# Tables and rows of the second and third expert asked for during the products of the expert before

## The chip, the core and the metric

The kernel runs on one core of a Trainium2 chip. The core has five engines that work from their own instruction streams and wait for each other on semaphores: PE (TensorE, matrix products; its weight loads are listed as PEld), DVE (VectorE), ACT (ScalarE), POOL (GpSimd) and SP (SyncE, which here only reads registers and issues DMAs). The metric is the device time of one execution in microseconds (us); less is better.

## The reference, cut to what matters

Attention with a small learned bias, then a dense MLP, then a mixture of experts with one expert for each token. Only the last part is touched by the change:

```python
def _moe2_ref(x, w_gate, w1, w2, capacity):          # x is 1152 x 512, 8 experts, capacity 288
    logits = x @ w_gate
    expert_idx = np.argmax(logits, axis=1)
    ...                                              # gate_w: softmax probability of the chosen expert
    for i in range(N):
        e = expert_idx[i]
        if counts[e] < capacity:
            disp[e, counts[e]] = x[i]
            ...
    h = np.maximum(np.einsum('ecd,edf->ecf', disp, w1), 0.0)     # 512 -> 1024
    y = np.einsum('ecf,efd->ecd', h, w2)                         # 1024 -> 512
    ...                                              # out[i] = gate_w[i] * y of the token's place, else 0
```

## The kernel before, in words

**Before the experts.** Attention and the dense MLP run in five row tiles, in an order written out in a list of numbers. They leave the MLP's output rows in a DRAM tensor `yscr` (1152 x 512), and a DRAM table `tbl` that gives, for each of the 8 experts and each of its 288 places, the token in the place and its gate weight. None of this is touched.

**The experts' order.** `experts_list` (DVE) makes a list `lst` of the experts that have tokens, with their count and the number `nf` of experts that are worked through in full. SP reads the list's entries into registers `ev[k]`, because the addresses of an expert's weights in DRAM depend on them. In this data the trace shows three experts worked in full (k = 0, 1, 2) and one more worked by a short path (`with_few`) beside the last.

**One expert, k.** `table(k)`: SP fetches the expert's 288 table entries into `tb` (96 x 3 x 2 numbers). `gather(k)`: DVE turns them into row numbers `gid`, and POOL issues three indirect DMAs, 96 rows of 2 KB each, from `yscr` into three tiles `XG`. `tokens(k)`: DVE makes the token numbers `tid` for the scatter at the end. `load1(k, i)` and `load2(k, i)`: SP fetches the two weight matrices in four pieces of 512 KB each, into `R1` and `R2` (shown as `AT` in the trace); a piece is fetched again for the next expert as soon as its last reader is done. `square`, `sized` and `halves` scale a piece by a power of two and split it into two float16 halves, `W1` and `W2`: the high half on ACT (on DVE for the fourth piece), the low half on DVE.

`gemm1(k)` is eight blocks of 12 matmuls (`ph`, `pt` <- `xT`, `W1`), with ACT and DVE making the two halves `HH` of each block's result. `gemm2(k)` is four blocks of 24 matmuls (`py` <- `HH`, `W2`). After its third block (dt = 2) PE turns the next expert's rows: `xt(k + 1, c)` transposes `XG[c]` into a bank, and ACT and DVE split that into `xT`, the moving operand of `gemm1(k + 1)`. `back` transposes a result back to rows, and `finish(k)`, which runs inside `gemm1(k + 1)`, ends it and issues the three scatters of the expert to `out` on POOL.

**What sets the order.** From the experts on there is no planner: each engine runs its instructions in the order of the code, `expert(0)` calling `gemm2(0)`, `expert(1)` calling `gemm1(1)`, `gemm2(1)` and so on, with a branch on `nf` between. Before the change, `table(k + 1)`, `gather(k + 1)` and `tokens(k + 1)` stand between `gemm1(k)` and `gemm2(k)`, and SP reads all of `ev[1]` to `ev[7]` and one more number ahead of `load1(1)`.

Of the kernel before, what the change touches and what calls it, by code (L numbers as in the profile page):

```python
# [25 lines left out]
E, F2 = 8, 1024  # L26
# [264 lines left out]
def tile_kernel(ctx: ExitStack, tc: tile.TileContext, a: dict, cap: int):  # L291
    nc = tc.nc
# [13 lines left out]
    def ts(eng, out, in0, s1, op0, s2=None, op1=ALU.bypass):  # L306
        eng.tensor_scalar(out=out, in0=in0, scalar1=s1, scalar2=s2, op0=op0, op1=op1)  # L307

    def stt(out, in0, s, in1, op0, op1, eng=None):
        (eng or dve).scalar_tensor_tensor(out=out, in0=in0, scalar=s, in1=in1, op0=op0, op1=op1)  # L310
# [36 lines left out]
    def cs(name, shape, dt=F32):  # L347
        return cst.tile(shape, dt, name=name)
# [841 lines left out]
    fl, lst, W = cs("fl", [1, E + 3]), cs("lst", [1, E + 3], I32), {}  # L1190
    ev = [None] * E

    def load1(k, ct):
        sp.dma_start(R1[:, ct], a["m1"][bass.ds(ev[k], 1), P * ct:P * ct + P].rearrange("o p f -> (o p) f"))

    def load2(k, i):
        sp.dma_start(RW2[:, 2 * i:2 * i + 2], a["m2"][bass.ds(ev[k], 1), 2 * P * i:2 * P * i + 2 * P].rearrange("o (c p) n -> p (o c) n", p=P))
# [7 lines left out]
    def raw(m, i):  # L1205
        return RW2[:, 2 * i:2 * i + 2] if m else R1[:, i]

    def sca(k, m, i, n=1):
        return W["s"][:, k % 2, m, i:i + n]

    def square(k, m, i, junk):
        j = junk.bitcast(BF16)
        act.activation(j.rearrange("p (a b) -> p a b", a=2) if m else j, raw(m, i), AF.Square, accum_out=sca(k, m, i))
# [188 lines left out]
    def table(k):  # L1402
        sp.dma_start(tb[k % 3], tv[bass.ds(ev[k], 1)].rearrange("o p c w -> (o p) c w"))

    def gather(k):
        g_ = gid[k % 3]
        ts(dve, g_, tb[k % 3][:, :, 0], float(NT - 1), ALU.min)
        for c in range(NCH):
            pool.indirect_dma_start(out=XG[c], out_offset=None, in_=yscr, in_offset=bass.IndirectOffsetOnAxis(ap=g_[:, c:c + 1], axis=0))

    def tokens(k):
        dve.tensor_copy(tid[k % 3], tb[k % 3][:, :, 0])

    def summed(k, m):
        tsum(sca(k, m, 4), sca(k, m, 0, 4))

    def sized(k, m, bank):
        total(k, m, bank)
        size(k, m, bank[:, 0:P])

    def halves(k, m, i):
        dst = W2[:, :, 2 * i:2 * i + 2] if m else W1[:, :, i]
        if i > 2:
            ts(dve, dst[:, 0], raw(m, i), sca(k, m, 5), ALU.mult)
        else:
            act.activation(dst[:, 0], raw(m, i), AF.Identity, scale=sca(k, m, 5))  # L1426
        stt(dst[:, 1], raw(m, i), sca(k, m, 5), dst[:, 0], ALU.mult, ALU.subtract)
# [6 lines left out]
    P3 = ((0, 0), (0, 1), (1, 0))  # L1434

    def gemm1(k, more=True, between=None):
        b_ = bool(k)
        for ft in range(8):
            ps = (PH + PT)[ft % 4]
            seq = [(ct, wv, xv) for ct in range(4) for wv, xv in P3]  # L1440
            for i, (ct, wv, xv) in enumerate(seq):
                pe.matmul(ps[:, 0:SL], W1[:, wv, ct, P * ft:P * ft + P], XT[k % 2][:, xv, ct], start=i == 0, stop=i == 11)  # L1442
            act.activation(HH[:, 0, ft], ps[:, 0:SL], AF.Relu)
            if k and ft == 0:
                summed(k, 1)
            stt(HH[:, 1, ft], ps[:, 0:SL], 0.0, HH[:, 0, ft], ALU.max, ALU.subtract)
            if k and ft == 0:
                finish(k - 1)
            if k and ft == 1:
                sized(k, 1, PO[0])  # L1450
            if ft > 1 and ft < 6:
                halves(k, 1, ft - 2)
            if k and more and ft > 3:
                square(k + 1, 0, ft - 4, W["j"])
            if between:
                between(ft)
# [10 lines left out]
    def gemm2(k):  # L1467
        if k == 0:
            for i in range(4):
                square(1, 0, i, W["j"])  # L1470
        summed(k + 1, 0)

        for dt in range(4):
            ps = PY[dt % 2]
            for ft in range(8):
                for i, (wv, hv) in enumerate(P3):
                    pe.matmul(ps[:, 0:SL], W2[:, wv, ft, P * dt:P * dt + P], HH[:, hv, ft], start=ft == 0 and i == 0, stop=ft == 7 and i == 2)  # L1477
            act.activation(YT[:, dt], ps[:, 0:SL], AF.Copy, scale=sca(k, 0, 7))
            if dt == (k == 0):
                sized(k + 1, 0, PO[1])  # L1480
            if dt == 2:
                for c in range(NCH):
                    xt(k + 1, c, (PT + PH)[c % 4])
            if dt == 1 or dt == 2:
                halves(k + 1, 0, 2 * dt - 2)
                halves(k + 1, 0, 2 * dt - 1)
            if dt > 0:
                back(k, dt - 1)
            if dt > 1:
                square(k + 1, 1, 2 * dt - 4, W["j"])  # L1490
                square(k + 1, 1, 2 * dt - 3, W["j"])

    def finish(k):
        back(k, 3)
        for c in range(NCH):
            scatter(k, c)
# [56 lines left out]
    def with_few(k):  # L1553
        few_loads()
        few_rows()
        if k:
            gemm1(k, False, lambda ft: few_x() if ft == 6 else None)
        else:
            few_x()

        def between(c):
            if c < 2:
                few_h(c)
            if c:
                few_flip(c - 1)
        gemm2_last(k, between)
        few_y(0)
        few_y(1)
        act.activation(XG[0], PO[1][:CS], AF.Copy, scale=sel[:, 0, 1:2])
        pool.indirect_dma_start(out=a["out"], out_offset=bass.IndirectOffsetOnAxis(ap=tidf[:, 0:1], axis=0), in_=XG[0], in_offset=None, bounds_check=NT - 1, oob_is_err=False)  # L1570

    def last(k):
        if k:
            gemm1(k, False)
        gemm2_last(k)

    def expert(k):
        if k + 1 == E:
            last(k)
            return  # L1580
        def next_():
            if k:
                for i in range(4):
                    load1(k + 1, i)
                gemm1(k)
            table(k + 1)
            gather(k + 1)
            tokens(k + 1)
            for i in range(4):
                load2(k + 1, i)  # L1590
            gemm2(k)
            expert(k + 1)

        def end():
            with tc.If(nv > k + 1) as more:
                with_few(k)
            with more.Else():
                last(k)

        if k < 2:  # L1600
            with tc.If(nf > k + 1) as more:
                next_()
            with more.Else():
                end()
        else:
            with tc.If(nf < k + 2) as done:
                end()
            with done.Else():
                next_()
# [2 lines left out]
    experts_list()  # L1612
    ts(dve, hm[:, 0:1], tok[:CS, 0:1], float(HC), ALU.is_lt)
    ts(dve, hm[:, 1:2], tok[:CS, 0:1], float(HC), ALU.is_ge)
    for k in range(1, E):
        ev[k] = nc.values_load(lst[0:1, k:k + 1], engines=[mybir.EngineType.SP], min_val=0, max_val=E - 1)
    evf = [nc.values_load(lst[0:1, E + 2:E + 3], engines=[mybir.EngineType.SP], min_val=0, max_val=E - 1)]
    for i in range(4):
        load1(1, i)
    gemm1(0)  # L1620
    tokens(0)
    nv = nc.values_load(lst[0:1, E:E + 1], min_val=1, max_val=E)
# [59 lines left out]
```

## Time and profile before

| | us |
|---|---|
| median of 3 runs (542.69 to 548.86) | 543.06 |
| the profiled execution, its own time | 543.5 |
| its span, first to last instruction | 541.6 |

| engine | busy us | share of the span |
|---|---|---|
| PE | 495.9 | 92% |
| DVE | 434.3 | 80% |
| ACT | 394.8 | 73% |
| POOL | 38.7 | 7% |

The mean granted clock of PE over the span is 0.962 of full speed. Times in the rows below are counted from the first instruction of the span. A busy PE is not a PE at its peak: matmuls are pipelined, and their ends are modelled, so spacings are read from starts.

### The profile page before, as it was taken

How to read it: one execution, taken by the hardware profiler on the slowest of the kernel's cores; microseconds unless marked ns; L12 is line 12 of the kernel's file. 1: busy time of each engine (PE TensorE's matmuls, PEld its weight loads, DVE VectorE, ACT ScalarE, POOL GpSimd, SP SyncE). 2: the span in 40 equal slices, each digit the busy share in tenths (PEclk: the TensorE clock that was granted, in tenths of full speed). 3: DMA queues.
4: the chain of work that ended last, by engine and by line, in shares of the span. 5: the costliest groups of instructions: out<-in, count | busy, mean ns of one | idle time of the engine just before them, and what ended most of it. 6: DMA issues, size and time to landing. Idle time of an engine off the chain costs nothing.

```text
span 541.6 us, 11894 instructions
## 1 busy us (share of the span) xinstructions
PE 495.9 (92%) x4479; PEld 336.9 (62%) x4479; DVE 434.3 (80%) x1172; ACT 394.8 (73%) x807; POOL 38.7 (7%) x67
## 2 busy tenths in 40 slices
PE   4756988999999999999999999999998797979994
PEld 3311655776676764566788747898467575867551
DVE  7999899999988899999877865799978966748300
ACT  7999999999875899999987633467952276847210
POOL 1000010000000011000000000001003002222101
PEclk9896699999999999999999999999999898999998
DMA  8998777630010233456331021180011267594100
GB/s 311 404 356 300 250 275 251 227 111 1 12 62 1 88 130 45 149 177 215 114 98 53 2 71 39 26 327 2 0 70 32 73 193 252 168 309 176 45 15 19
DMA packets 28211, 73.78 MB, mean 136 GB/s; under 512 B 4838, under 2 KB 4966, under 8 KB 26096
## 3 DMA queue, kind: packets, MB, share of 16 engines
q1 hardware_dynamic: 26576, 69.21, 37.7%
q0 software_dynamic: 1568, 3.72, 2.4%
q8 instruction: 37, 0.61, 0.5%
q14 instruction: 30, 0.25, 0.2%
HBM read 55.27 MB, written 17.87 MB: 135 GB/s over the span
## 4 chain that ended last, share of the span: by engine, by line
PE 57%; DMA 20%; DVE 11%; ACT 7%; issue 4%; SPq 1%; POOL 0%; another core or an unknown queue 0%; POOLq 0%; DVEq 0%; ACTq 0%
PE pb L868 15%; DMA xg<-yscr,gid 13%; PE pb L835 11%; PE pb L727 6%; PE ps L835 6%; DMA rw<-wi 4%; PE pb L663 3%; PE pb L518 3%; PE ps L633 3%; PE ps L663 2%; ACT ra L655 2%; ACT ra L666 2%; DVE WOt L310 1%; PE ps L619 1%; DMA out<-OC,tid 1%
## 5 line engine op out<-in xcount | busy, mean ns | idle before, releaser
L835 PEld LDWEIGHTS <-WIt 128*128 128x128 f16 x960 | 85.2, 98 | 10.6 <-issue 1.0
L835 PE MATMUL pb<-PX,WIt 128*128 128x256 f16 (+1 forms) x648 | 69.0, 263 | 0.0
L868 PE MATMUL pb<-WOt,ra 128*128 128x512 f16 x204 | 48.1, 379 | 0.0
L518 PE MATMUL pb<-ra,w2s 128*32 128x512 f32 (+17 forms) x252 | 37.4, 519 | 7.9 <-ACT ra L507 3.5
L868 PE MATMUL pb<-WOt,rw 128*128 128x512 f16 x180 | 42.0, 379 | 0.0
L655 ACT ACTIVATE ra<-ra,rm 128x576 f32<-128x576 f32 x50 | 39.3, 789 | 2.0 <-DVE rm L654 1.6
L507 ACT ACTIVATE ra<-AT,stab 128x512 f32<-128x512 f32 (+17 forms) x62 | 38.6, 663 | 2.1 <-DVE stab L307 2.0
L310 DVE SCALAR_TENSOR_TENSOR W<-AT,wsc,W 128x1024 f16<-128x1024 f32 x24 | 30.5, 1281 | 7.7 <-ACT W L1426 6.7
L868 PEld LDWEIGHTS <-ra 128*128 128x128 f16 x204 | 19.8, 98 | 22.2 <-issue 0.9
L654 DVE CUSTOM_DVE_ANT_0 ra<-ps,ra 128x576 f32<-128x576 f32 x43 | 31.3, 752 | 2.5 <-PE ps L622 1.4
L727 PE MATMUL pb<-ra,AT 128*64 128x128 f32 (+1 forms) x540 | 32.5, 271 | 0.7 <-ACT ra L666 0.7
L1442 PEld LDWEIGHTS <-W 128*128 128x128 f16 x288 | 28.1, 98 | 7.8 <-DVE xT L1186 1.0
L835 PE MATMUL ps<-PX,WIt 128*128 128x256 f16 (+1 forms) x312 | 32.8, 260 | 0.0
L1054 POOL DMA_INDIRECT tbl<-pk,rm x9 | 11.1, 1233 | 265.0 <-DVE rm L1051 175.8
L868 PEld LDWEIGHTS <-rw 128*128 128x128 f16 x180 | 17.3, 98 | 20.5 <-issue 1.4
L727 PEld LDWEIGHTS pb<-ra,AT 128*64 128x64 f32 x540 | 27.9, 139 | 3.3 <-ACT ra L666 1.4
L532 ACT ACTIVATE rbe<-pb,rl 128x48 f32<-128x48 f32 (+25 forms) x64 | 28.6, 484 | 1.4 <-DMA bscr<-rbe 0.6
L310 DVE SCALAR_TENSOR_TENSOR rw<-rw 128x1024 int32<-128x1024 int32 x24 | 29.3, 1224 | 0.0
L663 PE MATMUL pb<-ident,ra 128*128 128x128 f32 x159 | 24.0, 286 | 3.3 <-ACT ra L655 2.6
L1477 PE MATMUL py<-HH,W 128*128 128x288 f16 x192 | 26.9, 301 | 0.0
L666 ACT COPY ra<-pb 128x384 f32<-128x384 f32 x49 | 22.5, 492 | 3.5 <-PE pb L663 2.9
L307 DVE TENSOR_SCALAR ra<-AT,stab 128x544 f32<-128x544 f32 (+16 forms) x56 | 23.2, 445 | 0.9 <-PE pb L868 0.9
(477 smaller groups left out, 1155.2 us busy)
## 6 DMA issues: line engine op xcount, KB each, us to landing
AT<-m SPq DMA_DIRECT2D x24, 512.0 KB, 5.0
bscr<-rbe SPq DMA_DIRECT2D x36, 295.5 KB, 2.5
rw<-wo SPq DMA_DIRECT2D x8, 1024.0 KB, 6.2
ra<-bscr SPq DMA_DIRECT2D x28, 288.0 KB, 3.8
rw<-wi SPq DMA_DIRECT2D x4, 1024.0 KB
WOt<-wi SPq DMA_DIRECT2D x4, 1024.0 KB, 11.4
AT<-k SPq DMA_DIRECT2D x4, 576.0 KB
out<-ra SPq DMA_DIRECT2D x9, 256.0 KB, 2.7
```

The costliest lines, as they stand in the source:

```text
L310: (eng or dve).scalar_tensor_tensor(out=out, in0=in0, scalar=s, in1=in1, op0=op0, op1=op1)
L507: on_act = lambda h_=h_, g=g: act.activation(h_.t[:, 0:dn], T[:, 0:dn], AF.Relu, bias=stab[:, g:g + 1])
L518: pe.matmul(ps.t[32 * c:32 * c + 32, 0:d1 - d0], w2s, hs[c].t[:, d0:d1], start=True, stop=True)
L532: op("ACT", c_act(n, 1, 50), lambda ends=ends: act.activation(*ends(), AF.Copy, scale=rl[:, blk:blk + 1]), r=[ps, "stab"], p=[be], alt=[(" ...
L654: op("DVE", c_dve(S), lambda i=i, own=own, m_=m_, b_=b_: dve.tensor_tensor_reduce(out=own(), in0=blk(s_.t[:, 960 * i:960 * i + S]), in1=bl ...
L655: op("ACT", c_act(S, 2), lambda i=i, m_=m_, col=col: act.activation(t_.t[:, S * i:S * i + S], t_.t[:, S * i:S * i + S], AF.Exp, bias=m_.t[ ...
L663: pe.transpose(pa.t[:, P * j:P * j + P], t_.t[:, 384 * n + P * j:384 * n + P * j + P], ident)
L666: op("ACT", c_act(384, 0, 55), lambda dst=dst, src=src: act.copy(dst(), src()), r=[pa], w=[("tT", it, ct, b, n)], hold=[t_], alt=[("DVE", ...
L727: pe.matmul(ov[64 * i:64 * i + 64, ct % 2, w * bb:w * bb + w], v_, t_.t[:, at + c0:at + c0 + w], start=n == 0, stop=n == 4)
L835: pe.matmul(ps.t[:, n * f_:n * f_ + n], WI[:, wv, ct, P * ft:P * ft + P], xt.t[:, xv, ct, 0:n], start=i == 0, stop=i == 11)
L868: pe.matmul(y_.t, gv()[:, g2, c:c + P], WO[:, wv, ft], **kw)
L1442: pe.matmul(ps[:, 0:SL], W1[:, wv, ct, P * ft:P * ft + P], XT[k % 2][:, xv, ct], start=i == 0, stop=i == 11)
```

## The change

`table(1)` and `load1(1)` are issued right after the first number, `ev[1]`, is read; the other numbers are read behind them. `gather` now ends with `tokens`. `gather(1)` stands inside `gemm1(0)`, in its fourth block (ft = 3). For k = 1 and on, `table(k + 1)` stands ahead of `load1(k + 1)`, and `gather(k + 1)` at the head of `gemm1(k)`. In `gemm1(0)` alone the high half of the fourth piece of `W2` goes from DVE to ACT.

```diff
     def gather(k):
...
             pool.indirect_dma_start(out=XG[c], ...)
+        tokens(k)
...
     def halves(k, m, i):
-        if i > 2:
+        if k and i > 2:
             ts(dve, dst[:, 0], raw(m, i), sca(k, m, 5), ALU.mult)
...
     def gemm1(k, more=True, between=None):
+        if k and more:
+            gather(k + 1)
         for ft in range(8):
...
             act.activation(HH[:, 0, ft], ps[:, 0:SL], AF.Relu)
+            if k == 0 and ft == 3:
+                gather(1)
...
         def next_():
             if k:
+                table(k + 1)
                 for i in range(4):
                     load1(k + 1, i)
                 gemm1(k)
-            table(k + 1)
-            gather(k + 1)
-            tokens(k + 1)
             for i in range(4):
                 load2(k + 1, i)
             gemm2(k)
...
-    for k in range(1, E):
+    ev[1] = nc.values_load(lst[0:1, 1:2], ...)
+    table(1)
+    for i in range(4):
+        load1(1, i)
+    for k in range(2, E):
         ev[k] = nc.values_load(lst[0:1, k:k + 1], ...)
...
-    for i in range(4):
-        load1(1, i)
     gemm1(0)
```

On SP, where the second expert's table (`tb_5231`) and its weights (`AT<-m`) are asked for, the kernel before has this, behind the eight reads of the list and the four issues of `load1(1)`, whose last is the first row:

```order
L1194 DMA AT<-m 128x1024
L1622 TENSOR_LOAD lst
L1622 ISA x2
L1623 TENSOR_LOAD lst
L1623 ISA x2
L1601 COMPARE_AND_BRANCH
L1403 ISA
L1403 DMA tb_5231<-tbl 96x3x2
L1197 ISA
L1197 DMA AT<-m 128x2x512
```

and the change this, from the first table (`tb_5230`) on:

```order
L1403 DMA tb_5230<-tbl 96x3x2
L1616 TENSOR_LOAD lst
L1616 ISA x2
L1403 ISA
L1403 DMA tb_5231<-tbl 96x3x2
L1194 ISA
```

The table has moved ahead of seven reads of the list, the two reads for the branch, the branch itself and the four weight pieces; the pieces have moved ahead of seven reads.

On POOL, from the last scatter into `tbl` to the gathers for the third expert (`gid_5235`), the kernel before has

```order
L1054 DMA tbl<-pk_166,rm_126 2304x2
L1622 TENSOR_LOAD lst
L1623 TENSOR_LOAD lst
L1601 COMPARE_AND_BRANCH
L1409 DMA xg_5223<-yscr,gid_5234 96x512
L1409 DMA xg_5224<-yscr,gid_5234 96x512
L1409 DMA xg_5225<-yscr,gid_5234 96x512
L1601 COMPARE_AND_BRANCH
L1459 DMA out<-OC,tid_5236 1152x512 x3
L1409 DMA xg_5223<-yscr,gid_5235 96x512
L1409 DMA xg_5224<-yscr,gid_5235 96x512
L1409 DMA xg_5225<-yscr,gid_5235 96x512
```

and the change

```order
L1409 DMA xg_5223<-yscr,gid_5234 96x512
L1409 DMA xg_5224<-yscr,gid_5234 96x512
L1409 DMA xg_5225<-yscr,gid_5234 96x512
L1625 TENSOR_LOAD lst
L1626 TENSOR_LOAD lst
L1602 COMPARE_AND_BRANCH x2
L1409 DMA xg_5223<-yscr,gid_5235 96x512
L1409 DMA xg_5224<-yscr,gid_5235 96x512
L1409 DMA xg_5225<-yscr,gid_5235 96x512
L1462 DMA out<-OC,tid_5236 1152x512 x3
```

The first three gathers have moved ahead of the reads and the branch, the next three ahead of the first expert's scatters.

On DVE, in `gemm1(0)` from its third block (`pt_5221`) on, the kernel before has

```order
L310 SCALAR_TENSOR_TENSOR HH<-pt_5221,HH 128x288
L310 SCALAR_TENSOR_TENSOR W_5211<-AT,wsc,W_5211 128x1024
L310 SCALAR_TENSOR_TENSOR HH<-pt_5222,HH 128x288
L310 SCALAR_TENSOR_TENSOR W_5211<-AT,wsc,W_5211 128x1024
L310 SCALAR_TENSOR_TENSOR HH<-ph_5215,HH 128x288
L310 SCALAR_TENSOR_TENSOR W_5211<-AT,wsc,W_5211 128x1024
L310 SCALAR_TENSOR_TENSOR HH<-ph_5216,HH 128x288
L307 TENSOR_SCALAR W_5211<-AT,wsc 128x1024
L310 SCALAR_TENSOR_TENSOR W_5211<-AT,wsc,W_5211 128x1024
L310 SCALAR_TENSOR_TENSOR HH<-pt_5221,HH 128x288
```

and the change

```order
L310 SCALAR_TENSOR_TENSOR HH<-pt_5221,HH 128x288
L310 SCALAR_TENSOR_TENSOR W_5211<-AT,wsc,W_5211 128x1024
L307 TENSOR_SCALAR gid_5234<-tb_5231 96x3
L1413 CAST tid_5237<-tb_5231 96x3
L310 SCALAR_TENSOR_TENSOR HH<-pt_5222,HH 128x288
L310 SCALAR_TENSOR_TENSOR W_5211<-AT,wsc,W_5211 128x1024
L310 SCALAR_TENSOR_TENSOR HH<-ph_5215,HH 128x288
L310 SCALAR_TENSOR_TENSOR W_5211<-AT,wsc,W_5211 128x1024
L310 SCALAR_TENSOR_TENSOR HH<-ph_5216,HH 128x288
L310 SCALAR_TENSOR_TENSOR W_5211<-AT,wsc,W_5211 128x1024
L310 SCALAR_TENSOR_TENSOR HH<-pt_5221,HH 128x288
```

The two small instructions on the table stand between the third and the fourth block, and the 128x1024 `TENSOR_SCALAR` is gone from DVE.

## Rows read from the trace of the kernel before

**Rows 1.** Waits of PE from 429 us on: line, released by: us, times, longest.

```profile
PE pt L1431 <- DMA xg<-yscr,gid: 4.4, 4, 2.1
PE ph L1431 <- DMA xg<-yscr,gid: 1.2, 2, 0.9
...
PE po L1216 <- DVE wsc L327: 0.3, 1, 0.3
```

**Rows 2.** Timeline, PE, second expert's rows: start, us, what [idle before <-releaser].

```profile
448.27 3.10 PE L1477 MATMUL py<-HH,W 128*128 128x288 f16 x24
453.48 0.55 PE L1431 MATMUL pt<-ident,xg 96*128 96x96 f32 x4 [2.11 <-DMA xg<-yscr,gid]
454.38 0.55 PE L1431 MATMUL pt<-ident,xg 96*128 96x96 f32 x4 [0.35 <-DMA xg<-yscr,gid]
455.19 0.59 PE L1431 MATMUL ph<-ident,xg 96*128 96x96 f32 x4 [0.26 <-DMA xg<-yscr,gid]
455.57 0.84 PE L1464 MATMUL po<-ident,YT 128*96 128x128 f32 x3
456.21 4.46 PE L1477 MATMUL py<-HH,W 128*128 128x288 f16 x24
...
462.31 0.49 PE L1464 MATMUL po<-ident,YT 128*96 128x128 f32 x3
```

**Rows 3.** Timeline, PE, behind the third expert's rows.

```profile
487.99 3.95 PE L1477 MATMUL py<-HH,W 128*128 128x288 f16 x24
...
493.57 0.49 PE L1464 MATMUL po<-ident,YT 128*96 128x128 f32 x3
```

**Rows 4.** Windows: us, busy PE, PEld, DVE, ACT, POOL, PEclk, DMA, GB/s.

```profile
401.00:402.00 1.00, 0.53 (x6) 0.44 (x4) 0.50 (x3) 0.56 (x1) 0.00 (x0) 1.00 0.44 172
...
456.00:458.00 2.00, 2.00 (x10) 1.31 (x9) 1.23 (x3) 2.00 (x3) 0.00 (x0) 0.50 0.37 141
```

**Rows 5.** SP: reads of the list (last figures: first and last start), and DMA issues.

```profile
L1616 SPq TENSOR_LOAD <-lst x7: 262/266/289, 432.3 to 435.8; - x7
...
437.08 2.75 SPq L1194 DMA_DIRECT2D AT<-m  x4
441.31 0.33 SPq L1403 DMA_DIRECT2D tb<-tbl  x1
461.21 0.33 SPq L1403 DMA_DIRECT2D tb<-tbl  x1
```

**Rows 6.** The small tables (tile tb), three of them, from issue to landing.

```profile
DMA to landing us min/median/max: 3.2/4.2/5.3
```

**Rows 7.** The gathered rows (tile xg), from issue to landing.

```profile
DMA to landing us min/median/max: 2.4/5.7/8.3
```

**Rows 8.** Timeline, DVE and POOL, around the tables and the gathers.

```profile
435.61 1.28 DVE L310 SCALAR_TENSOR_TENSOR W<-AT,wsc,W 128x1024 f16<-128x1024 f32 x1 [0.58 <-ACT W L1426]
442.28 0.82 DVE L310 SCALAR_TENSOR_TENSOR HH<-pt,HH 128x288 f16<-128x288 f32 x2
446.60 0.17 DVE L307 TENSOR_SCALAR gid<-tb 96x3 uint32<-96x3 int32 x1 [3.44 <-DMA tb<-tbl]
447.72 0.92 POOL L1409 DMA_INDIRECT xg<-yscr,gid  x1 [25.93 <-DMA AT<-m]
473.24 1.80 POOL L1459 DMA_INDIRECT out<-OC,tid  x1 [3.65 <-DMA out<-OC,tid]
```

**Rows 9.** Timeline, ACT and DVE, between the waits and the next product.

```profile
451.96 0.50 ACT L1478 ACTIVATE YT<-py,wsc 128x288 f32<-128x288 f32 x1 [0.74 <-PE py L1477]
456.20 1.14 ACT L1426 ACTIVATE W<-AT,wsc 128x1024 f16<-128x1024 f32 x1
459.36 1.28 DVE L310 SCALAR_TENSOR_TENSOR W<-AT,wsc,W 128x1024 f16<-128x1024 f32 x1
482.72 0.50 ACT L1478 ACTIVATE YT<-py,wsc 128x288 f32<-128x288 f32 x1
487.98 1.14 ACT L1426 ACTIVATE W<-AT,wsc 128x1024 f16<-128x1024 f32 x1
```

More of the change, by code (lines that the diff above doesn't have):

```diff
@@ L1436, in gemm1 @@
     def gemm1(k, more=True, between=None):
-        b_ = bool(k)
+        if k and more:
+            gather(k + 1)
         for ft in range(8):
             ps = (PH + PT)[ft % 4]
-            seq = [(ct, wv, xv) for ct in range(4) for wv, xv in P3]
-            for i, (ct, wv, xv) in enumerate(seq):
+            for i, (ct, wv, xv) in enumerate([(ct, wv, xv) for ct in range(4) for wv, xv in P3]):
                 pe.matmul(ps[:, 0:SL], W1[:, wv, ct, P * ft:P * ft + P], XT[k % 2][:, xv, ct], start=i == 0, stop=i == 11)
             act.activation(HH[:, 0, ft], ps[:, 0:SL], AF.Relu)
+            if k == 0 and ft == 3:
+                gather(1)
             if k and ft == 0:
@@ L1614, in tile_kernel @@
     ts(dve, hm[:, 1:2], tok[:CS, 0:1], float(HC), ALU.is_ge)
-    for k in range(1, E):
+    ev[1] = nc.values_load(lst[0:1, 1:2], engines=[mybir.EngineType.SP], min_val=0, max_val=E - 1)
+    table(1)
+    for i in range(4):
+        load1(1, i)
+    for k in range(2, E):
         ev[k] = nc.values_load(lst[0:1, k:k + 1], engines=[mybir.EngineType.SP], min_val=0, max_val=E - 1)
     evf = [nc.values_load(lst[0:1, E + 2:E + 3], engines=[mybir.EngineType.SP], min_val=0, max_val=E - 1)]
-    for i in range(4):
-        load1(1, i)
     gemm1(0)
```

## The prediction

> **What bounds the kernel now.** PE is busy for 92% of the span, so I first looked for the places where it is not: the waits of PE from the first product of the experts on. There are few. Six waits for the gathered rows `xg` come to 4.4 + 1.2 = 5.6 us, and one on a small sum is 0.3 [rows 1]. Everything else in this stretch is PE at work. So the change can only be worth what hangs on these waits, and the timeline tells how much that is.
>
> At the second expert, the third block of `gemm2(0)` ends at 448.27 + 3.10 = 451.37, and the first transposes of `xg` start at 453.48; the three groups waited 2.11, 0.35 and 0.26, together 2.72 [rows 2]. The 24 matmuls behind them took 4.46 where the 24 before took 3.10: same work, lower clock. The window over them shows a granted clock of 0.50, the lower level of 1.2 GHz, with PE fully busy [rows 4]; before it PE had stood and transposed for four us. So a second price hangs on the wait. At the third expert it is the same picture: the other three waits are 5.6 - 2.72 = 2.88, and the 24 matmuls took 3.95 [rows 3].
>
> Why the rows come late: `gather(1)` needs its table. SP asked for it at 441.31, behind eight reads of the list and the 2 MB of `load1(1)` issued from 437.08 on [rows 5]; `gid` could start at 446.60, after DVE had idled 3.44 for it, and POOL issued the first gather at 447.72 [rows 8]. Three gathers later PE needed it.
>
> **The change, part by part.** *SP.* Seven reads start between 432.3 and 435.8, six steps, so one is 0.58 [rows 5]. The table of the second expert is now asked for after one of them, at about 433.0 instead of 441.31. The four weight pieces lose seven reads (4.1) and gain one issue (about 0.6, twice the 0.33 of the issue itself): about 433.6 instead of 437.08. What is queued behind them, `load2(1)`, has the same instructions ahead of it as before, so it stays where it was.
>
> *The first gather.* A table landed 3.2 to 5.3 after its issue [rows 6]; so it is there between 436.2 and 438.3. DVE comes to `gid` when the low half of the first piece is done, 435.61 + 1.28 = 436.89 [rows 8]. That is a new wait on DVE, of 0 to 1.4. Queued behind it are the `HH` halves and `W2`, for which PE waits in `gemm2(0)`. I take it as nothing: DVE gives up a 128x1024 `TENSOR_SCALAR` in the same stretch, so its last `HH` (442.28) comes no later; without that cover it would cost up to 1.4. The move of that instruction to ACT costs nothing: ACT waits for PE between its `HH` there. From `gid` to the first gather took 1.12 (446.60 to 447.72), and each issue is 0.92 with a small gap, so the third starts at 440.5 to 442. Gathers landed 2.4 to 8.3 after issue [rows 7]: 442.9 to 450.3 at the latest, before PE's 451.37. The wait goes.
>
> *The second gather.* Its table is asked for behind `load2(1)`, at about 445 instead of 461.21 [rows 5], and lands by 450.3. DVE comes to `gid` at the head of `gemm1(1)`, right behind `W1` (458.4, below), about 459. Three gathers, 3.6 us of POOL, then stand ahead of the three scatters of the first expert; those are waited for by the next writer of `OC`, which comes a whole `gemm2` later, so this is covered. The rows land by 471 at the latest (462.5 + 8.3) and are needed behind the block whose `YT` was at 482.72 [rows 9], some 4 us earlier now, near 479. The wait goes.
>
> *What is late next.* Without the waits PE would save at the second expert 2.72, the clock 4.46 - 3.10 = 1.36, and half of the 0.64 between 455.57 and 456.21, which ran at the lower clock too: 4.40. But the next product also needs `W1`, and that hangs on ACT: after `YT` (451.96) it has three splits of `xT`, then the high half of the third piece, at 456.20; DVE's last low half ends at 459.36 + 1.28 = 460.64, 4.44 later [rows 9]. Without the waits ACT needs four instructions of 0.50 from 451.96, an estimate: it reaches the high half at 454.0, and `W1` is complete at 458.4 instead of 460.64. The first block ended at 462.31 [rows 2], 1.67 after `W1`; now it can end right behind it, 458.6. That gives 3.7, or up to 4.40 if ACT is quicker; one more DVE instruction guards the bank that comes next, so the low bound is 3.2. I take 3.6. At the third expert PE saves 2.88 + 0.85 = 3.73, and ACT's chain (482.72 + 2.0 = 484.7, plus 4.44 = 489.1) ends well before the block's end would be, 493.57 - 3.73 = 489.84 [rows 3, 9]; with some of the transposes at the lower clock too I take 3.8, bounds 3.2 and 4.2.
>
> *The small sum.* The 0.3 of PE hangs on squares of `load1(1)`'s pieces, which now land 3.5 earlier: 0.3, bounds 0 and 0.3.
>
> **The sum.** 3.6 + 3.8 + 0.3 = 7.7. The span of 541.6 becomes 533.9, and the profiled execution's own 543.5 becomes 535.8. The median of the runs is 0.44 below that execution, so I forecast 535.4. Bounds of the costs alone: 6.4 to 8.9, that is 534.2 to 536.7. Behind the third expert everything is in order on PE and shifts as a whole.
>
> **The rivals.** *The clock falls all the same.* The transposes stay (three groups and one more, 1.5 us), and PE may be taken down by them alone. Against it: in the window at 401 PE was busy for 0.53 of 1 us and the clock stayed at 1.00 [rows 4]. If so, 1.36 + 0.32 and 0.85 come back, 2.5 at most: 537.9. Chance 0.11.
>
> *One of the waits stays.* The gathers now compete with the weight loads of another moment, and 8.3 was seen. One whole term is then lost: 539.2. Chance 0.07.
>
> *POOL is held by DVE.* The first gathers are issued while DVE has no pause, from 435.61 to 443.1 (442.28 + 0.82). A scatter issued under such work took 1.80 instead of 0.92 [rows 8]; at that rate the third gather starts at 443 and lands by 451.5, still no loss, since its group is the third on PE. Were POOL shut out until 443.1, the third would start at 445.5 and land by 453.8, 1.7 behind the third group's turn: 537.1. The 1.80 speaks for a stretch and against a shut door; chance 0.04. The Trainium skill, SBUF — State Buffer, section "Who interferes with whom", states the harder form: DVE and GpSimd share a port pair as an exclusive lock, and while DVE runs in a two-port mode the other blocks fully. By that rule the time would be the 537.1; the trace's 1.80 agrees only in that the issue gets longer.
>
> *Slower.* `gid` of the third expert stands in front of all of `gemm1(1)`'s work on DVE. If its table landed late, DVE and then PE would stand, us for us. It decides from a landing at 459 + 7.7 = 466.7 on. Were SP to reach it only where it was before, 461.21 + 5.3 = 466.5, the gain would be gone: 543. It would need SP to be held behind `load2(1)` for 16 us; its order puts nothing long there. Chance 0.05, 0.03 of it for over 2%.
>
> **How the numbers follow.** 0.68 for the forecast with its bounds, 0.11, 0.07, 0.04 and 0.05 for the rivals, 0.05 for more than the bounds. The range reaches from a little under the lowest bound, since single runs lie some tenths apart, to the case of one wait that stays: 533.0 to 539.6, about 0.9 of the chance. A measurement of this kernel can tell about 2% from no change, 10.9 us, so faster means under 532.2. All the waits together and their clock are less than that: faster 0.05, same 0.92, slower 0.03.
>
> **What would show it.** In the profile of the change: the table issued near 433 and `gid` near 437 on DVE; no wait of PE on `xg`; the 24 matmuls behind the transposes at about 3.1; `gemm1(1)` starting near 457 and waiting shortly for DVE's `W`. It is wrong if PE still waits on `xg`, if the clock is 0.50 there, or if DVE idles long before `gid`.

## The result and the profile after

The change takes 535.61 us (median of 4 runs, 534.81 to 536.87) against 542.88 of the kernel before beside it (541.32 to 548.86): ratio 0.987, 95% interval 0.983 to 0.991. (The 548.86 is one execution in a slower state, and the ratio leaves it out.) The forecast was 535.4, range 533.0 to 539.6, and no change beyond 2%. The profiled execution took 534.81 itself, the fastest of the four; its span is 532.9 where it was 541.6.

PE no longer waits for the rows. These are all of its waits in the change from the first product of the experts on (line, released by: us, times, longest), in place of [rows 1]:

```profile
PE ph L1443 <- DVE A L307: 0.7, 1, 0.7
PE po L1467 <- DVE OC L1468: 0.5, 2, 0.3
PE ph L1443 <- DVE W L310: 0.5, 1, 0.5
```

The timeline of PE in the change, from the first expert's second product on (start, us, what [idle before <- releaser]); the lines answer to [rows 2], the last two to [rows 3]:

```profile
441.09 6.04 PE L1480 MATMUL py<-HH,W 128*128 128x288 f16 x48
447.22 0.49 PE L1216 MATMUL po<-ident,wsc 128*128 128x128 f32 x2
...
450.81 0.82 PE L1432 MATMUL pt<-ident,xg 96*128 96x96 f32 x8
...
452.13 3.10 PE L1480 MATMUL py<-HH,W 128*128 128x288 f16 x24
...
455.40 1.51 PE L1443 MATMUL ph<-xT,W 128*128 128x288 f16 x11
457.38 0.30 PE L1443 MATMUL ph<-xT,W 128*128 128x288 f16 x1 [0.47 <-DVE W L310]
457.94 0.51 PE L1467 MATMUL po<-ident,YT 128*96 128x128 f32 x3 [0.26 <-DVE OC L1468]
...
479.48 3.10 PE L1480 MATMUL py<-HH,W 128*128 128x288 f16 x24
...
484.95 0.51 PE L1467 MATMUL po<-ident,YT 128*96 128x128 f32 x3 [0.26 <-DVE OC L1468]
```

The transposes of `xg` follow the block before them (447.87 + 3.10) without a gap, the 24 matmuls behind them take 3.10 at both experts, and what PE waits for now is `W1` and `OC`, both from DVE. The granted clock (PEclk) stays up, as the window over the transposes shows (us, busy PE, PEld, DVE, ACT, POOL, PEclk, DMA, GB/s); just behind them [rows 4] had 0.50:

```profile
450.00:452.00 2.00, 2.00 (x22) 1.85 (x21) 2.00 (x2) 1.81 (x4) 0.00 (x0) 1.00 0.19 55
```

The queues of the change, SP, then DVE and POOL, with the landings behind them (for [rows 5] to [rows 8]):

```profile
428.77 4.53 SPq L1403 DMA_DIRECT2D tb<-tbl  x2
433.48 1.95 SPq L1194 DMA_DIRECT2D AT<-m  x4
443.49 0.34 SPq L1403 DMA_DIRECT2D tb<-tbl  x1
...
436.62 0.16 DVE L307 TENSOR_SCALAR gid<-tb 96x3 uint32<-96x3 int32 x1
441.44 0.81 DVE L310 SCALAR_TENSOR_TENSOR HH<-pt,HH 128x288 f16<-128x288 f32 x2
458.18 0.15 DVE L307 TENSOR_SCALAR gid<-tb 96x3 uint32<-96x3 int32 x1
...
437.71 1.48 POOL L1409 DMA_INDIRECT xg<-yscr,gid  x1 [16.11 <-ACT HH L1444]
439.50 1.25 POOL L1409 DMA_INDIRECT xg<-yscr,gid  x1 [0.31 <-issue]
441.05 1.25 POOL L1409 DMA_INDIRECT xg<-yscr,gid  x1 [0.30 <-issue]
459.09 0.91 POOL L1409 DMA_INDIRECT xg<-yscr,gid  x1 [16.79 <-DVE wsc L327]
...
DMA to landing us min/median/max: 1.8/1.8/8.2
DMA to landing us min/median/max: 4.7/5.7/6.9
DMA to landing us min/median/max: 3.1/3.2/3.4
```

The second expert's table is the later of the two issues that end at 433.30; neither `gid` has an idle time in front of it. The last three lines are the landings of the tables, of the second expert's rows and of the third's.

**A ruler for the runs.** The part ahead of the experts moves by some 4 us from execution to execution (last section), and with it every total. So the tables below also count from A, the start of the first expert's second product, to B, the first row behind the second expert's first block (462.31 in [rows 2]), and to C, the same point at the third expert (493.57 in [rows 3]). A of the kernel before is this line of its PE timeline:

```profile
441.27 6.04 PE L1477 MATMUL py<-HH,W 128*128 128x288 f16 x48
```

so A to B is 21.04 and A to C 52.30. In the change they are 457.94 - 441.09 = 16.85 and 43.86: 4.19 won at the second expert, 4.25 more at the third, 8.44 of the 8.7 of the span. Four more traces in which nothing between A and C should differ (the change twice more, and the two runs that fill PE ahead of A) gave 43.86 each.

The 52.30 is less sure. It is one trace, in which the first product of the experts ran fast (3.12 for its first 24 matmuls). In all 13 comparisons of this document the medians differ from those of the kernel before (542.54 to 542.93) by less than A to C does, by 0.2 to 2.2, on average 1.3. A likely reason: before the change SP asks for the second expert's table without waiting for PE, so when the first product runs slow, A moves and the table hardly does, and the wait behind A shrinks. e1 and e4 below show that; a second trace of the kernel before, which would show it there, was not taken.

### The profile page after: what moved, and what is told of

Same layout as the page of the kernel before. It is cut to its first block, busy times and chain, and to the rows that moved or that the text cites. A ratio compares the mean times of both kernels' runs of the same rounds, so it can differ in the third digit from the quotient of the medians.

```text
span 532.9 us, 11895 instructions
## 1 busy us (share of the span) xinstructions
PE 492.6 (92%) x4479; PEld 335.6 (63%) x4479; DVE 432.4 (81%) x1171; ACT 394.2 (74%) x808; POOL 37.8 (7%) x67
## 4 chain that ended last, share of the span: by engine, by line
PE 57%; DMA 19%; DVE 13%; ACT 7%; issue 3%; POOL 0%; SPq 0%; POOLq 0%; DVEq 0%; ACTq 0%
PE pb L868 16%; PE pb L835 12%; DMA out<-OC,tid 10%; PE pb L727 6%; DMA xg<-yscr,gid 6%; PE ps L835 6%; PE pb L663 3%; DMA rw<-wi 3%; PE pb L518 3%; PE ps L633 3%; PE ps L663 2%; ACT ra L655 2%; DVE rw L310 2%; ACT ra L666 2%; DVE rw L307 1%
## 5 line engine op out<-in xcount | busy, mean ns | idle before, releaser
L1480 PE MATMUL py<-HH,W 128*128 128x288 f16 x192 | 24.7, 286 | 0.0
```

## Experiments

Each ratio is to runs of the kernel before beside that run; A to B and A to C are from the one trace of each.

| run | edit | median | ratio to before, 95% | A to B | A to C |
|---|---|---|---|---|---|
| before | | 542.88 | | 21.04 | 52.30 |
| the change | | 535.61 | 0.987 (0.983-0.991) | 16.85 | 43.86 |
| e1 | second expert put back | 539.06 | 0.993 (0.989-0.997) | 19.82 | 48.45 |
| e2 | third expert put back | 541.72 | 0.998 (0.995-1.001) | 16.85 | 50.04 |
| e3 | tables early, gathers back | 541.44 | 0.997 (0.993-1.000) | 17.41 | 51.00 |
| e4 | before, with the waits filled | 541.82 | 0.997 (0.993-1.001) | 18.93 | 49.42 |
| e5 | the change again | 535.75 | 0.988 (0.985-0.992) | 16.85 | 43.86 |
| e6 | third table late | 541.03 | 0.998 (0.995-1.002) | 16.86 | 48.36 |
| e7 | high half of `W1` on ACT | 536.28 | 0.989 (0.986-0.992) | 16.29 | 43.78 |
| e8 | gather behind the scatters | 538.66 | 0.994 (0.991-0.996) | 16.86 | 47.93 |
| e9 | high half of `W2` back on DVE | 536.13 | 0.986 (0.982-0.990) | 16.84 | 43.85 |
| e10 | longer fill ahead of the experts | 535.84 | 0.986 (0.983-0.990) | 16.84 | 43.86 |
| e11 | and two short fills | 536.12 | 0.987 (0.983-0.990) | 16.85 | 43.86 |
| e12 | the change again | 535.17 | 0.987 (0.983-0.990) | 16.84 | 43.86 |

### Is the gain the sum of two terms? (e1, e2)

```diff
 # e1: list reads, table(1) and load1(1) in their old order; and
-            if k == 0 and ft == 3:
-                gather(1)
...
+            else:
+                table(1)
+                gather(1)
             for i in range(4):
                 load2(k + 1, i)
 # e2: for k = 1 and on
-        if k and more:
-            gather(k + 1)
...
             if k:
-                table(k + 1)
                 for i in range(4):
                     load1(k + 1, i)
                 gemm1(k)
+                table(k + 1)
+                gather(k + 1)
```

> The second expert's table, list reads and gather are put back to where they stood, the third expert's stay early. Theory (two separate terms that add): the gain at the second expert, about 4.2 by the two traces (4.0 and 0.2 of the small sum), is lost and the third's 4.25 stays: 539.8 (539.0 to 540.6), PE waits for xg some 2.7 at the second expert and none at the third, the 24 matmuls behind the second expert's rows at about 4.4. Rival (the later stages absorb an early delay): 536 to 537. Rival (the early rows of the second expert carry the whole gain): 543.

> The third expert's table and gather are put back, the second expert's stay early. Theory: the 4.25 of the third expert is lost, the second's 4.2 stays: 539.9 (539.0 to 540.8), PE waits for xg some 2.9 in three at the third expert only, the 24 matmuls behind them at about 3.9. Rival (the third expert's wait was only the second's, carried on): 535.6.

Each part alone brings less than its share: A to C is 3.85 shorter with the third alone (e1), 2.26 with the second alone (e2), 8.44 with both. e1's total fell where it was forecast, e2's did not. e2 kept the 4.19 up to B (16.85), but from B to C it took 33.19, where the kernel before took 31.26 and the change 27.01. PE in e2, at the third expert's rows:

```profile
478.58 3.10 PE L1478 MATMUL py<-HH,W 128*128 128x288 f16 x24
482.89 0.55 PE L1432 MATMUL pt<-ident,xg 96*128 96x96 f32 x4 [1.21 <-DMA xg<-yscr,gid]
484.95 0.90 PE L1432 MATMUL pt<-ident,xg 96*128 96x96 f32 x4 [1.50 <-DMA xg<-yscr,gid]
486.58 0.90 PE L1432 MATMUL ph<-ident,xg 96*128 96x96 f32 x4 [0.73 <-DMA xg<-yscr,gid]
...
487.91 4.94 PE L1478 MATMUL py<-HH,W 128*128 128x288 f16 x24
```

Counted from A, PE came to the block ahead of the rows 4.17 earlier than before (479.57 and 478.58), and the three groups of rows 4.04, 3.44 and 3.25 earlier (landing 8.0 to 8.8 after issue, before 8.1 to 8.3). So it waited 3.44 instead of 2.88. That is 0.56 of the 1.93 given back; the 24 matmuls, 4.94 instead of 3.95, are another 0.99, and the transposes and `back` at the lower clock the rest. In this trace nearly half of what the second expert won was lost at the third, and most of that to the clock.

e1 is two things at once. Its first product ran slower (3.92 for the first 24 matmuls), so SP asked for the table 0.77 ahead of A (the kernel before: 0.04 behind it), PE waited 1.69 instead of 2.72 (the 24 matmuls behind took 4.40), and 1.22 was won up to B that the edit had not left there. And it stood 1.23 for `HH` once, behind an ACT that stood 3.5 in `gemm1(1)`; what held ACT I did not find, and no other run shows it. Without that the third expert's part alone is 2.63 + 1.23 = 3.86, near its 4.25.

### The table or the gather? (e3)

```diff
-            if k == 0 and ft == 3:
-                gather(1)
...
                 gemm1(k)
+            gather(k + 1)
             for i in range(4):
                 load2(k + 1, i)
```

> The tables and the first weights stay early on SP, but both gathers go back behind the first product, where they stood in the code. Theory: at the second expert the table was what came late (in the kernel before DVE idled 3.44 for it), so gid starts near 442.3 and not 446.6, the third gather is issued near 446 and PE's wait shrinks from 2.7 to at most 0.7; at the third expert the table was there in time, the place of the gather behind the first product and the scatters made it late, so its 2.9 and the slow 24 matmuls stay. Together 539.8 (539.5 to 541). Rival (the tables are all that matters): 535.6. Rival (the gather's place decides at both): 543.

At the second expert the early table is nearly everything: `gid` stands right behind DVE's reads for the branch, with no wait for its table, and PE has no wait on `xg`. A to B is 17.41, 0.56 more than in the change. At the third nothing is won: the table had long been there, `gid` came behind all of `gemm1(1)` on DVE, PE waited 3.65 for the rows, and the 24 matmuls behind them were the slowest of all runs. DVE and PE in e3:

```profile
444.02 0.17 DVE L307 TENSOR_SCALAR gid<-tb 96x3 uint32<-96x3 int32 x1 [0.62 <-issue]
...
480.38 0.55 PE L1432 MATMUL pt<-ident,xg 96*128 96x96 f32 x4 [0.36 <-DMA xg<-yscr,gid]
483.31 0.55 PE L1432 MATMUL pt<-ident,xg 96*128 96x96 f32 x4 [2.38 <-DMA xg<-yscr,gid]
484.77 0.90 PE L1432 MATMUL ph<-ident,xg 96*128 96x96 f32 x4 [0.91 <-DMA xg<-yscr,gid]
...
486.10 5.50 PE L1476 MATMUL py<-HH,W 128*128 128x288 f16 x24
```

The mechanism was as expected at both experts; the total missed by the same effect as e2's, a longer wait and a slower group at the third expert. The early table is what counts at the second expert, the early gather at the third (whose table must be there for it, see e6).

### What the clock alone is worth (e4)

```diff
                 for c in range(NCH):
+                    for i in range((8, 7, 7)[c] if k else (17, 2, 2)[c]):
+                        pe.matmul(PH[1][:, 0:SL], W2[:, 0, i % 8, P * dt:P * dt + P], HH[:, 0, i % 8], start=True, stop=True)
                     xt(k + 1, c, (PT + PH)[c % 4])
```

> The kernel before, in which PE runs 21 and 22 more 128x288 matmuls (0.12 each), whose result nobody reads, where it waits for the second and the third expert's rows; everything else is unchanged. It tells the price of the clock from that of the wait. Theory (the stretch of standing takes the clock down): the granted clock stays at 1.00, the 24 matmuls behind the rows take 3.10 instead of 4.46 and 3.95; W1 is complete at 460.64 as before, so the block behind it ends near 460.8 instead of 462.31, 1.5 less, and 0.9 less at the third expert: 540.6 (540.0 to 541.8). Rival (the transposes take the clock down by themselves): 24 matmuls still at 4.46 and 3.95, 543. Rival (clock stays, but W1 sets the end whatever the clock): 3.10 and 543.

The matmuls behind the rows took 3.10 at both experts. PE and, second, DVE in e4:

```profile
444.50 6.04 PE L1477 MATMUL py<-HH,W 128*128 128x288 f16 x48
447.74 0.17 DVE L307 TENSOR_SCALAR gid<-tb 96x3 uint32<-96x3 int32 x1 [1.36 <-DMA tb<-tbl]
...
458.12 3.10 PE L1477 MATMUL py<-HH,W 128*128 128x288 f16 x24
...
486.58 0.55 PE L1431 MATMUL pt<-ident,xg 96*128 96x96 f32 x4 [0.60 <-DMA xg<-yscr,gid]
...
488.61 3.10 PE L1477 MATMUL py<-HH,W 128*128 128x288 f16 x24
```

The third expert is the clean case: counted from A, its second group of rows came 1.86 earlier than before (485.21 and 486.58) and PE to the block ahead of them 2.10 earlier (479.57 and 480.70), so the wait to be filled was no shorter; one of 0.60 was left, and the granted clock was 1.00 from 484 to 490. With the change's own window, where the transposes ran at 1.00 with nothing beside them, this leaves the standing as what takes the clock down here.

A to C fell by 2.88 (2.11 and 0.77; 1.5 and 0.9 were expected), but the 2.11 is not the clock alone. The first product ran slow in this trace (4.81), SP asked for the table at 442.02, 2.48 ahead of A, and `gid` began 3.24 behind A instead of 5.33. `W1` was complete 1.06 earlier from A (462.81 - 444.50 = 18.31, before 460.64 - 441.27 = 19.37). Taking that off leaves 1.05, so by this estimate the clock is worth between a fifth (1.05 + 0.77) and a third (2.88) of the 8.44. The totals alone (0.993 to 1.001) can't tell it from nothing.

### Where the change would have gone wrong (e6, e8)

```diff
 # e6
-                table(k + 1)
                 for i in range(4):
                     load1(k + 1, i)
+                table(k + 1)
 # e8
-        if k and more:
-            gather(k + 1)
...
                 finish(k - 1)
+                if more:
+                    gather(k + 1)
```

> The change, with the third expert's table asked for behind the four pieces of load1(2) and not ahead of load2(1). This makes the rival that ended on the slower side. Theory: SP issues the table some 17 after the start of the second product (458 in the change's trace) instead of 2.4 after, it lands 1.8 to 8.2 later, and DVE stands at gid until then, 1.7 to 8; PE stands too, less about 1, since the small sum and HH are queued behind gid on DVE. Median of the landings 5: about 4 lost, 539.6 (536.5 to 542.5), and the 24 matmuls of the stretch may lose their clock besides. Rival (DVE has enough slack there): 535.6.

> The change, with the gather of the third expert's rows put behind the three scatters of the first expert on POOL (and one block later on DVE). Theory: the order of POOL has slack both ways. The third scatter is issued about 25.7 after the start of the second product, so the gathers go at 27 to 29.5, land 3 to 8 later, 30 to 37.5, and PE wants them at 37.1 to 37.7: 535.6 (535 to 537). Rival (only ahead of the scatters they are in time): waits of PE on xg of 1 to 3 and a lower clock, 538 to 540.

e6 is the rival on the slower side, with a smaller delay. DVE and PE in e6:

```profile
464.17 0.17 DVE L307 TENSOR_SCALAR gid<-tb 96x3 uint32<-96x3 int32 x1 [3.92 <-DMA tb<-tbl]
...
464.52 0.79 PE L1216 MATMUL po<-ident,wsc 128*128 128x128 f32 x2 [2.61 <-DVE wsc L327]
465.11 4.46 PE L1443 MATMUL pt<-xT,W 128*128 128x288 f16 x24
```

DVE stood 3.92 at `gid`, PE 2.61 behind it, and then the clock was down for 24 matmuls (4.46 for 3.10): 4.50 lost of A to C. The late table cost more here than the 3.92 that DVE stood for it.

e8 shows how little room the third expert's gathers have; my expectation fell. POOL, the landing of the third expert's rows, and PE, in e8:

```profile
466.27 1.85 POOL L1462 DMA_INDIRECT out<-OC,tid  x1 [2.76 <-DMA out<-OC,tid]
468.43 1.71 POOL L1409 DMA_INDIRECT xg<-yscr,gid  x1 [0.30 <-PE pt L1441]
...
471.67 0.92 POOL L1409 DMA_INDIRECT xg<-yscr,gid  x1 [0.30 <-PE po L1216]
DMA to landing us min/median/max: 7.1/8.3/9.6
...
481.34 0.55 PE L1432 MATMUL ph<-ident,xg 96*128 96x96 f32 x4 [2.02 <-DMA xg<-yscr,gid]
482.05 4.77 PE L1480 MATMUL py<-HH,W 128*128 128x288 f16 x24
```

The scatters wait for each other's landing, two issues took 1.85 and 1.71, and the last gather went out 31.1 from A where I had 29.5. More than that, its rows took 7.1 to 9.6 to land, in the change 3.1 to 3.4. What differs is the traffic around them: the change's third gathers (459.09 on) go out ahead of `load2(2)`, which SP issues from 464.43 on; in e8 they go out behind it. It is so in the other traces too: 8.1 to 8.3 in the kernel before, 8.0 to 8.8 in e2, 8.9 in e3 and 6.5 to 8.3 in e4 behind them, 3.0 to 3.3 in e6 ahead of them. That the weights cause it is read from these cases; no run isolates it. So the place ahead of the scatters is worth 4.07 (47.93 for 43.86), nearly the third expert's whole term.

### What waits now, and the small edit (e7, e9)

```diff
 # e7
-        if k and i > 2:
+        if k and m and i > 2:
 # e9
-        if k and i > 2:
+        if i > 2:
```

> The change, with the high half of the fourth piece of W1 made on ACT for every expert, as the change does for W2 of the first. It is meant to take away what PE waits for now: 0.47 for W1 and 0.26 for OC at the second expert, 0.26 at the third. Theory: W1 is complete 0.75 earlier, these waits go, but ACT comes to the four squares 1.1 later and the small sum of W2 becomes the wait: net gain 0 to 1.0, 535.2 (534.4 to 536.2). Rival (ACT is the bound there): slower by up to 1, 536.6.

> The change, with the high half of the fourth piece of W2 back on DVE at the first expert. Theory: DVE's last HH of the first product ends 0.75 later, near 442.25 + 0.75 = 443.0 as in the kernel before, where PE did not wait for it either; nothing moves: 43.86 on PE from the start of the second product to the third expert's point, 535.7 (535 to 536.5). Rival (that instruction was the cover for the two small ones on the table, and without it PE waits for HH or W2): 0.7 to 1.4 more, 536.4 to 537.1, with a wait of PE on HH or W early in the second product.

In e7 the waits for `W1` and `OC` went (A to B 16.29); instead PE waited 0.35 for ACT's `YT` at both experts, and right behind it the small sum became the wait, 0.41, since ACT comes to its squares later: the 24-matmul group behind C starts 46.52 after A (491.33 - 444.81), in the change 45.89 (486.98 - 441.09). 536.28 is no gain over the 535.75 of the change beside it. e9 changed nothing between A and C (43.85), so the instruction taken off DVE was no part of the gain.

### Keeping the clock up ahead of the experts (e10, e11, e5, e12)

```diff
 # e10: the matmuls that the kernel already runs unread ahead of the rows
-            for i in range(22):
+            for i in range(34):
 # e11: also 3 and 6 of them inside the next group
```

> The change, with 34 instead of 22 of the matmuls that nobody reads and that the kernel already runs ahead of the first expert's rows, so that PE does not stand there (it waited 1.51 behind them, twelve take 1.47). Theory (standing takes the clock down, as at the second and third expert): in the traces of the change and its variants the granted clock was 0.50 to 0.71 in the stretch behind this wait, and in some of them the first 24 matmuls of the experts took 5.4 and not 3.1. With the longer fill the clock stays up more often: 1.0 gained always in that stretch, and up to 2.3 where the clock had been down: 534.3 (533 to 535.8). Rival (the clock there is set by the small matmuls with their waits behind it): 535.7.

> As the run before it, with 3 and 6 more of the unread matmuls in the two waits of 0.41 and 0.84 that follow. Theory: PE stands for no more than 0.7 at a time from there to the first product, the clock stays at 1.00, the matmuls between 426 and 428 take half of their time, and the first 24 of the experts 3.1 in every execution: 533.7 (532.5 to 535.2). Rival (the fill delays what PE waits for, or the clock falls all the same): 535.7 to 536.5.

> The change itself once more, beside the three that follow: 535.6 (534 to 537). From the start of the second product of the first expert to the first block behind the third expert's rows it took 43.86 on PE, and 52.30 in the kernel before; if the theory of the stage holds, this number comes again within 0.5, whatever the part of the program ahead of the experts does.

> The change itself beside the three runs before, so that they are compared with it on the same chip: 535.7 (535 to 537), 43.86 on PE from the start of the second product to the third expert's point.

No gain: 535.84 and 536.12 beside 535.17 of the change. PE in e10:

```profile
429.04 4.79 PE L1443 MATMUL ph<-xT,W 128*128 128x288 f16 x24 [2.21 <-DVE A L307]
```

Five matmuls of the group behind the fill took 0.78 in e10 (from 425.43) and 1.40 in the three traces of the change. But they took 0.78 in e3 and e9 too, without the longer fill, so that the fill kept the clock up there is not shown. In these three PE then stood 2.21 for DVE, and the first 24 matmuls took 4.78 or 4.79. In e11 the short fills ran behind the two waits, at 426.78 and 427.58, and not in them. Nothing found here beats the change.

## Why the prediction was right, step by step

**The queues** went as worked out: table issued at 432.96 (433.0 forecast), `gid` at 436.62 (436.89), the second `gid` at 458.18 (459). The new wait of DVE on its table, taken as nothing within 0 to 1.4, did not show: the table landed 1.8 after its issue, faster than the 3.2 to 5.3 of [rows 6]. The third expert's table, asked for at 443.49 (about 445), took 8.2, longer than any of [rows 6]; it was there by 452, 6 ahead of its `gid`.

**The first gather.** The third issue ran from 441.05 to 442.30 (forecast to start between 440.5 and 442), the rows took at most 6.9 more, and PE came at 450.81. e3 adds that the table, not the gather's place, was what bound there.

**The second gather** was in time for the reason given, and sooner: the step let the rows land by 471 with the 8.3 of before, they landed 3.4 after issue at most, by 466. That the rows land faster there was no part of the reasoning, and was not needed: with 8.3 they would still have come 7 ahead of PE (478.16). Behind the scatters (e8) the last gather goes out so late that its landing decides: after 3.4 it would have come at 476, ahead of PE's turn near 478, after 9.6 it did not, and the term was gone.

**Second expert**, 3.6 forecast. The trace gives 4.19, with the small sum's 0.22 (6.35 to 6.13 from A to its row; 0.3 forecast) 3.97 without it. Up to the start of the 24 matmuls (456.21 and 452.13, from A 14.94 and 11.04) 3.90 was saved, 3.68 without the small sum, where 2.72 + 0.32 was counted. Most of the 0.64 between them are the transposes of `xg`, which had run at the lower clock too, and which the step left out. `W1` then gave back 1.07 where the step had 4.40 - 3.6 = 0.8: the 24 matmuls were 1.36 quicker, and of that (21.04 - 14.94) - (16.85 - 11.04) = 0.29 was left at B. Its chain ran a little earlier than forecast and through DVE rather than ACT; DVE and ACT in the change, for [rows 9]:

```profile
452.52 1.17 ACT L1427 ACTIVATE W<-AT,wsc 128x1024 f16<-128x1024 f32 x1
...
456.04 1.28 DVE L310 SCALAR_TENSOR_TENSOR W<-AT,wsc,W 128x1024 f16<-128x1024 f32 x1
```

ACT had the high half at 452.52 (454.0 forecast), and the last low half ended at 457.32 (458.4).

**Third expert**, 3.8 within 3.2 to 4.2: measured 4.25, just above its bound. The statement that ACT's chain ends well before the block there was wrong: 0.26 for `OC` and a stretched block (12 matmuls of 1.95 instead of 1.63) show the same DVE chain. From `W1` and `OC` 0.74 of the 0.85 of the quicker matmuls was given back (from their start to C 5.58 before, 5.47 now). What made up for it were again the slow transposes: from the block ahead of the rows to the 24 matmuls PE took 8.42 before and 4.26 now, 4.16 less, of which 2.88 are the waits. So the step had one term at nothing that cost 0.74 and counted little of another that brought 1.28, and its 3.8 came out close in part by luck.

**The sum** of 7.7 came out as 8.7 of the span and 7.3 between the medians (542.88 and 535.61). That the forecast lies within 0.3 of the median is in part luck: the two traces gave 0.7 more than the sum from A to C, and the totals gave less than the traces did. The forecast reckoned from the one trace of the kernel before, as if its A to C were that of every execution. Adding the two terms was right for the change; for the second expert's part alone it would have been wrong, since without the third's e2 lost 6.18 and not 4.25 (50.04 - 43.86).

**The rivals.** *The clock falls all the same* is out by the change's window and by e4. *One wait stays* did not happen; e8 shows what it would have cost (538.66, where the rival had 539.2). *POOL is held by DVE*: the first three issues took 1.48, 1.25 and 1.25, under DVE's work, against 0.91, and with one more 128x1024 `TENSOR_SCALAR` of DVE in that stretch (e9) 1.48, 1.60 and 1.69. POOL in e9:

```profile
439.68 1.48 POOL L1409 DMA_INDIRECT xg<-yscr,gid  x1 [17.79 <-DMA AT<-m]
441.46 1.60 POOL L1409 DMA_INDIRECT xg<-yscr,gid  x1 [0.30 <-issue]
443.37 1.69 POOL L1409 DMA_INDIRECT xg<-yscr,gid  x1 [0.30 <-issue]
```

The issues are stretched; in the change all three were out by 442.30, which is when DVE's work ends (441.44 + 0.81), and not shut out until then. The Trainium skill, SBUF — State Buffer, section "Who interferes with whom", states that DVE in a two-port mode and GpSimd take a shared port pair as a lock: whoever issues first has it for the whole instruction, and the other blocks fully; the trace agrees in that the issues got longer, here by 0.3 to 0.8 each, and does not show them shut out until DVE paused. *Slower* worked as described (e6), except that the clock is lost on top of the delay.

## What to carry to other kernels

When two waits of the same kind follow each other, removing the first one brings the engine to the second one sooner; price each alone and both together, since the second can take back a part of the first one's gain (1.93 of 4.19 in e2). A wait of PE costs more than its length if the matmuls behind it run at the lower clock: look at the group behind each wait, and price its transposes too. And an early place for a gather can be worth more than the time it is early: ahead of the weight loads it landed in about 3 here, behind them in 6.5 to 9.6. Last, a stretch measured from one engine's mark is only as steady as everything that does not follow that engine: A to C came back within 0.01 in the change, and in e1 and e4, where the second expert's table stood late, it hung on how fast the first product had run.

## What the hardware showed that was not expected

The first 24 matmuls of the experts took between 3.11 and 5.50 in traces whose code up to there is the same. PE's timeline in e12 (the change), and then in e7:

```profile
429.73 3.11 PE L1443 MATMUL ph<-xT,W 128*128 128x288 f16 x24 [0.58 <-DVE xT L1186]
```

```profile
430.65 5.50 PE L1443 MATMUL ph<-xT,W 128*128 128x288 f16 x24 [0.55 <-DVE A L307]
```

The waits right ahead of them are alike (0.58 and 0.55), the granted clock is not: 1.00 from 430 on in e12, 0.50 from 426 to 434 in e7. The two had parted earlier, at the 22 unread matmuls, which took 2.86 in e12 and 4.49 in e7, though both were at 0.50 from 426 to 428; what decides it no run shows. With A between 440.53 and 444.81 in all traces, this is why totals of a few runs could not tell effects of 2 to 3 us apart and the stretch from A to C, which came back within 0.01 for the change, could. How steady it is where the clock falls inside it, one trace of each run can't show.

A table of 2.3 KB landed 1.8 after its issue twice and 8.2 once in the same execution; the 8.2 is the third expert's, issued at 443.49 behind the weights of `load2(1)` (7.2 and 8.0 in e12 and e5; in e6, where it alone is moved, 4.3). The Trainium skill, SBUF — State Buffer, section "The DMA setup-cost knee (why "@ 1 MiB" ≠ asymptote)", puts a roughly fixed 2 us on each transfer; the trace agrees for the two that were issued with no weights queued ahead of them.
